# Sliding-window attention beside a gated linear unit: row maxima sent two units later, a second scratch buffer, and another order inside the PV burst

## The chip, the core and the metric

The kernel runs on one core of one Trainium2 chip. What is measured is the device time of one execution in microseconds (us). A core has a matrix engine (TensorE, PE in the profile; PEld is its weight load), a vector engine (VectorE, DVE), a scalar engine (ScalarE, ACT), a general engine (GpSimd, POOL), and a queue that issues nearly all DMAs here (SyncE, SP). Each engine executes its own list of instructions in order and waits on semaphores for the others.

## The reference

Two branches share the input x (2048 rows of 512) and are mixed row by row by a gate.

```python
def _A_ref(x, wqkv, wo):
    H = 32; Dh = 16; W = 256
    q, k, v = ...                                   # x @ wqkv, 32 heads of 16
    scores = jnp.einsum("bhqd,bhkd->bhqk", q, k) * (Dh ** -0.5)
    mask = (idx[:, None] - idx[None, :] >= 0) & (idx[:, None] - idx[None, :] < W)
    p = _softmax(jnp.where(mask, scores, -1e9))
    return einsum("bhqk,bhkd->bhqd", p, v) ... @ wo

def _B_ref(x, w_gate, w_up, w_down):                # F = 1376
    return (_sigmoid(x @ w_gate) * (x @ w_up)) @ w_down

g = _sigmoid((x * gate_w).sum(-1, keepdims=True))
return g * a + (1 - g) * b
```

Everything is float32. A query sees itself and the 255 keys before it, so a block of 128 queries needs three blocks of 128 keys.

## The kernel before, in words

The 32 heads are taken in 8 groups of 4, the 2048 rows in 16 blocks of 128. One pair (head group, block) is a *unit*; units are numbered `u` from 0 to 127, and the main loop runs over them and a few more. Four consecutive units are a *group of maxima* with index `s`, 32 in all. The engines' order is the order in which this Python loop emits instructions: TensorE, VectorE, ScalarE and SyncE are not reordered.

In the loop, unit `u` does the following:

- `s_part(u, hh)`, for each of the four heads `hh`: the scores of query block `u` with its three key blocks, queries on partitions (tile `s`, two PSUM buffers). VectorE adds the mask and takes the row maximum (L314); the elementwise result goes into a scratch tile `junk` that nobody reads, the maximum into `mx`.
- `st_part(u - 9, hh)`: the transposed scores of key block `u - 9` with query blocks `u - 9` to `u - 7` (tile `st`, three PSUM buffers). Here the contraction has extra rows, in which the query side carries minus the row maximum, so that the exponential on ScalarE (L360) comes out shifted. Block `u - 7` is thus the newest whose maximum is read. A key block at the end of a head group reads only up to that group's end.
- For this the maxima of four units are turned into ring rows. `max_split(s)` makes a high and a low part and transposes them on VectorE (L324, L325, L329, tiles `nm` and `nt`); `max_store(s)` writes them to DRAM with four DMAs (L335); `max_load(s)` reads them back into row 0 of the `ring`'s 32-row strips with one DMA (L340).
- `pv_burst(w, n)`: probabilities times values for `n` query blocks at once (four, near the end two), at the head of unit `w + n + 10`: that is every unit with `u % 4 == 2` in the steady part. Each matmul uses a tile of 64 rows by 32 columns of the array: two halves of the key rows (`half`) times four heads. `acc[0]`, tag `s`, collects the first half, `acc[1]`, tag `st`, the second. Key halves `k` have different widths, from 64 to 320 query columns. `o_take` then copies one half out on ScalarE (L422), adds the other on VectorE (L425), and appends four `oT` stores and one of the sums to the list `later`.
- Fill work: `run_slots` emits matmuls of the gate and up projections (`gu`) and of later q/k projections (`pj`) between the attention matmuls, the two row halves offset against each other. Their results are copied out and appended to `later` as `gu_scratch` stores.
- SyncE's list in a unit: `max_store` if due, then all that `later` holds from the unit before, then up to three DMAs that build the next `ring` stack (`sdma`: copies from `sh` and `sl`), then `max_load` if due. `sdma` is filled with thirteen DMAs in units with `u % 8 == 1`.

After the attention part the down projection and the output projection follow; the change does not touch them.

Of the kernel before, what the change touches and what calls it, by code (L numbers as in the profile page):

```python
# [7 lines left out]
F32 = mybir.dt.float32  # L8
# [6 lines left out]
P = 128  # L15
# [9 lines left out]
NB = T // P  # L25
# [3 lines left out]
VW = DH + 1  # L29
VROW = H * VW  # L30
GW = HG * VW
# [25 lines left out]
def gated_mix_kernel(  # L57
# [14 lines left out]
    mm = nc.tensor.matmul  # L72
# [34 lines left out]
    NU = NG * NB  # L107
# [20 lines left out]
    with ExitStack() as actx:  # L128
# [169 lines left out]
        def s_part(u, hh):  # L298
            g, i = divmod(u, NB)
            s = g * NC + i // 4  # L300
            if i % 4 == 0 and hh == 0:
                mxs[s] = spool.tile([P, HG, 4], F32, tag="mx", name=f"mx{s}")
            k0 = max(0, i - 2)
            tag = "st" if u < LAG and hh >= 2 else "s"
            pt = ps.tile([P, 3 * P], F32, tag=tag, name=f"s{u}_{hh}", bufs=2 if tag == "s" else 3)
            lhsT = blk(g, i, hh, 0)
            for k, e in pieces(g, k0, i + 1):
                mm(  # L308
                    pt[:, (k - k0) * P:(e - k0) * P], lhsT, blk(g, k, hh, 1, e - k),
                    start=k == k0, stop=e == i + 1, skip_group_check=True,  # L310
                )
            n = (i + 1 - k0) * P
            junk = spool.tile([P, 3 * P], F32, tag="junk", name=f"junk{u}_{hh}", bufs=1)
            nc.vector.tensor_tensor_reduce(  # L314
                junk[:, 0:n], pt[:, 0:n], mask[:, 3 * P - n:], scale=1.0, scalar=NEG,
                op0=ALU.add, op1=ALU.max, accum_out=mxs[s][:, hh, i % 4:i % 4 + 1],
            )
# [3 lines left out]
        def max_split(s):  # L321
            mx = mxs.pop(s)
            nm = spool.tile([P, HG, 2, 4], F32R, tag="nm", name=f"nm{s}")
            nc.vector.tensor_scalar(nm[:, :, 0], mx, -1.0, None, op0=ALU.mult)  # L324
            nc.vector.scalar_tensor_tensor(  # L325
                nm[:, :, 1], mx, -1.0, nm[:, :, 0].bitcast(F32), op0=ALU.mult, op1=ALU.subtract,
            )
            nms[s] = spool.tile([P, QB], F32, tag="nt", name=f"nt{s}")
            nc.vector.transpose(nms[s], nm.bitcast(F32).rearrange("p h l b -> p (h l b)"))  # L329
# [14 lines left out]
        pts = {}  # L344
# [40 lines left out]
        def pv_burst(u, n):  # L385
            g, i = divmod(u, NB)
            acc = [
                ps.tile([P, CH], F32, tag=tag, name=f"pv{tag}{u}", bufs=bufs)
                for tag, bufs in (("s", 2), ("st", 3))
            ]  # L390
            span = {
                k: (max(0, 64 * k), min(n * P, 64 * k + 5 * 64))
                for k in range(-4, 2 * n) if i + k // 2 >= 0
            }
            order = [
                sorted((k for k in span if k % 2 == half), key=lambda k: (span[k][0] - span[k][1], k))
                for half in range(2)
            ]
            for m in range(len(order[0])):
                for hh in range(HG):  # L400
                    for half in range(2):
                        k = order[half][m]
                        j = i + k // 2
                        q0, q1 = span[k]
                        o = -(k // 2) * P
                        r = slice(64 * half, 64 * half + 64)
                        c = j * GW + hh * VW
                        mm(  # L408
                            acc[half][32 * hh:32 * hh + 32, q0:q1],
                            vg[g % 2][r, c:c + 32], pts[g * NB + j][r, hh, q0 + o:q1 + o],  # L410
                            start=m == 0, stop=m == len(order[0]) - 1, skip_group_check=True,
                            tile_position=(64 * half, 32 * hh),
                        )
            o_take(g, i, n, acc)

        def o_take(g, i, n, acc):
# [212 lines left out]
        for u in range(N):  # L629
            if u == LAG:  # L630
                vctx.close()
                ppool = actx.enter_context(tc.tile_pool(name="ppool", bufs=1))
                for k in range(2):
                    vg.append(ppool.tile([P, NB * GW + 16], F32, name=f"vg{k}"))
                    nc.gpsimd.memset(vg[k][:, NB * GW:], 0.0)
                hvs += [
                    v.rearrange("p (w t) -> p w t", t=CH)
                    for v in [vg[0][:, 0:2 * CH]] + [region[:, o:o + 2 * CH] for o in HVO]
                ]
            if u == LAG + 1 or u % NB == 0 and 0 < u < NU:  # L640
                v_load(u // NB)
            if u == 4:
                load_gu(0, 0)
                load_gu(0, 1)
            if u % 8 == 1 and u > 8 and u // 8 + 1 < NP:
                sdma = stack_build(u // 8 + 1)
            if u % 16 == 8 and u // 16 + 2 < NG:
                raw_q = load_wqk(u // 16 + 2)
            if u % 4 == 0 and 0 < u <= NU:
                max_store(u // 4 - 1)  # L650
            run_dmas(later)
            later.clear()
            run_dmas(sdma[:SD])
            del sdma[:SD]
            if u % 4 == 1 and 1 < u <= NU + 1:
                max_load(u // 4 - 1)
            if WD <= u < WD + 16 and (u - WD) % 2 == 0:
                load_d((u - WD) // 2)
            s4 = {1: 4, 5: 5, 9: 6, U_LAST: NSTEP - 2, U_LAST + 1: NSTEP - 1}.get(u)
            if u % 4 == 3 and u > LAG and (u + 2) // 4 + 4 < NSTEP - 2:  # L660
                s4 = (u + 2) // 4 + 4
            if s4 is not None:
                if u < LAG:
                    (work if u == 1 else first).append((3 * ND, lambda k, s4=s4: proj_mm(s4, k), lambda s4=s4: proj_post(s4)))
                else:
                    work.append(proj_group(s4))
            if u == NU + PVLAG - 1:
                hold_group(*rest.pop(0))
            for hh in range(HG):
                if hh == 0 and u % 2 == 0:  # L670
                    if u in bursts:
                        pv_burst(*bursts[u])
                if hh == 0:
                    head = min(2, bursts.get(u, (0, 0))[1] // 2)
                    run_slots(head)
                if u < NU:
                    s_part(u, hh)
                if 0 <= u - LAG < NU:
                    st_part(u - LAG, hh ^ 1 if u < NU else hh)
                if u < LAG:  # L680
                    flush(behind)
                else:
                    if behind:
                        behind.pop(0)()
                    if acts:
                        acts.pop(0)()
                if u >= LAG and (hh < HG - 1 or u % 2 == 0 if u < NU else hh % 2 == 1):
                    run_slots((GAP if u < NU else 2 * GAP) - (hh < head if u < NU else head * (hh == 1)))
            if u < LAG - 1:
                done += run_first(n_first * (u + 1) // LAG - done)  # L690
            elif u < LAG:
                run_first(n_first - done - 3 * ND)
                split_gu(0, 0)
                split_gu(0, 1)
                flush(acts)
                flush(behind)
                run_first(3 * ND)
                done = 0
            if u % 4 == 3 and u < NU:
                max_split(u // 4)  # L700
            if u // 16 + 2 < NG:
                if u % 16 == 13:
                    acts.append(lambda g=u // 16 + 2, r=raw_q: (
                        split_wqk(g, r, 0), behind.append(lambda: split_wqk(g, r, 1))))
            if 0 <= u - LAG < NU:
                mask_p(u - LAG)
            if WD + 2 <= u < WD + 10 and (u - WD) % 2 == 0:
                acts.append(lambda f=(u - WD) // 2 - 1: split_d(f, True))
            if SUMS <= u and (u - SUMS) % 4 == 0:
                sums_load((u - SUMS) // 4)  # L710
            if SUMS + 2 <= u and (u - SUMS) % 4 == 2:
                behind.append(lambda c=(u - SUMS) // 4: later.append(sums_invert(c)))
            if u >= HLOAD and (u - HLOAD) % 2 == 0:
                h_load((u - HLOAD) // 2)
            if u >= N - 2:
                flush(acts)
                flush(behind)
                h_skew(u - N - 1)
# [162 lines left out]
```

## Time and profile before

| | |
|---|---|
| median of 3 runs | 766.97 us (766.41 to 768.11) |
| profiled execution | 765.99 us, span 764.3 us |
| busy: TensorE, VectorE, ScalarE, GpSimd | 745.9, 483.6, 434.9, 163.7 us |
| share of the last chain: TensorE, VectorE | 81%, 9% |
| `junk` reductions (L314) | 512, 270.8 us busy |
| `pv` matmuls (L408) | 2880, each in two float32 passes counted apart: 1440 on `pvs`, 1440 on `pvst` |

The span runs from the first to the last instruction. "Busy" is time in which at least one instruction of the engine runs; a busy TensorE can still have one half of its rows empty. The attention part, where all of the change lies, goes from about 40 to 590 us.

### The profile page before, as it was taken

Reading aid. Unit: us, or ns where it says so; the run is one execution under the profiler, and the core shown is the slowest. Engines: PE = TensorE matmul, PEld = TensorE weight load, DVE = VectorE, ACT = ScalarE, POOL = GpSimd, SP = SyncE. Lnnn points to the kernel's source line nnn. Section 1 sums busy time; section 2 is a strip of 40 time slices with the busy share of each in tenths; the row PEclk is TensorE's granted clock in tenths of the full one; section 3 lists DMA queues with packets and bytes.
Section 4 is the critical chain, followed back from the end, with each engine's and each line's share of the span. In section 5 each row is a group of like instructions: output and inputs, shape, how many; then the busy total and the mean of one; then the engine's idle time right before and its main releaser. Section 6 shows DMA issues by size and latency. Waiting matters only on the chain.

```text
span 764.3 us, 20558 instructions
## 1 busy us (share of the span) xinstructions
PE 745.9 (98%) x7652; PEld 592.4 (78%) x7652; DVE 483.6 (63%) x1429; ACT 434.9 (57%) x900; POOL 163.7 (21%) x256
## 2 busy tenths in 40 slices
PE   8999999999999999999999999999999999999997
PEld 6877777877877777878787777878877778888886
DVE  5356767766676766777667677577612794739371
ACT  5412666666576666666656666666665673625341
POOL 7000322233133232323223322332331000000000
PEclk9999999999999999999999999999999999999999
DMA  8373544445344455344543525643366776648351
GB/s 301 93 240 123 143 123 116 124 114 158 118 117 128 122 138 140 101 135 113 148 140 99 149 66 144 165 123 107 101 196 186 234 245 224 185 142 269 110 163 55
DMA packets 88787, 112.69 MB, mean 147 GB/s; under 512 B 36082, under 2 KB 45810, under 8 KB 88688
## 3 DMA queue, kind: packets, MB, share of 16 engines
q1 hardware_dynamic: 88688, 111.39, 49.7%
q8 instruction: 60, 0.98, 0.6%
q14 instruction: 39, 0.32, 0.1%
HBM read 49.72 MB, written 36.45 MB: 113 GB/s over the span
## 4 chain that ended last, share of the span: by engine, by line
PE 81%; DVE 9%; DMA 4%; SPq 3%; issue 2%; ACT 1%; DVEq 0%; ACTq 0%
PE gu L240 29%; PE pvs L408 8%; PE pj L240 7%; PE s L308 7%; PE st L355 4%; PE pd L81 4%; PE pd L79 4%; PE pd L80 4%; DVE junk L314 4%; PE vps L79 2%; SPq L282 2%; PE vps L80 2%; PE vps L81 2%; PE pa L79 2%; PE pa L81 2%
## 5 line engine op out<-in xcount | busy, mean ns | idle before, releaser
L314 DVE CUSTOM_DVE_ANT_0 junk<-s,mask 128x384 f32<-128x384 f32 (+2 forms) x512 | 270.8, 529 | 157.5 <-PE st L355 74.8
L240 PE MATMUL gu<-xh,w 64*128 64x512 f32 (+3 forms) x1384 | 353.7, 394 | 0.4 <-ACT sp L501 0.3
L360 ACT ACTIVATE region<-st 128x384 f32<-128x384 f32 (+2 forms) x512 | 237.9, 475 | 126.2 <-PE st L355 71.9
L240 PE MATMUL gu<-xl,w 64*128 64x512 f32 (+3 forms) x692 | 243.8, 394 | 0.0
L240 PEld LDWEIGHTS gu<-xh,w 64*128 64x128 f32 (+3 forms) x1384 | 203.6, 183 | 16.6 <-ACT sp L501 1.4
L308 PE MATMUL s<-ring 64*128 64x384 f32 (+2 forms) x536 | 168.0, 338 | 10.7 <-DVE mx L314 9.3
L355 PE MATMUL st<-ring 64*128 64x384 f32 (+2 forms) x536 | 169.1, 334 | 0.0
L365 POOL TENSOR_SCALAR_AFFINE_SELECT region<-region 128x512 f32<-128x512 f32 x128 | 82.9, 648 | 362.0 <-ACT region L360 305.6
L308 PEld LDWEIGHTS s<-ring 64*128 64x128 f32 x536 | 94.0, 184 | 56.3 <-DVE mx L314 45.1
L240 PEld LDWEIGHTS gu<-xl,w 64*128 64x128 f32 (+3 forms) x692 | 124.5, 183 | 9.7 <-issue 1.6
L355 PEld LDWEIGHTS st<-ring 64*128 64x128 f32 x536 | 94.7, 184 | 6.1
L240 PE MATMUL pj<-xh,wqh 64*128 64x512 f32 (+1 forms) x232 | 93.4, 405 | 1.0 <-ACT xh L75 1.0
L240 PE MATMUL pj<-xl,wqh 64*128 64x512 f32 (+1 forms) x232 | 91.8, 399 | 0.0
L408 PE MATMUL pvs<-region,vg 64*32 64x320 f32 (+4 forms) x1440 | 74.5, 346 | 0.0
L408 PE MATMUL pvst<-region,vg 64*32 64x320 f32 (+4 forms) x1440 | 73.1, 341 | 0.0
L240 PE MATMUL pj<-xh,wql 64*128 64x512 f32 (+1 forms) x232 | 72.5, 398 | 0.0
L370 POOL TENSOR_SCALAR_AFFINE_SELECT region<-region 128x512 f32<-128x512 f32 x112 | 71.5, 638 | 0.0
L81 PE MATMUL pd<-ring,hb 128*128 128x512 f32 (+1 forms) x176 | 69.4, 394 | 0.7 <-DVE hb L76 0.7
L408 PEld LDWEIGHTS pvs<-region,vg 64*32 64x32 f32 x1440 | 49.7, 106 | 26.0 <-issue 9.6
L79 PE MATMUL pd<-ring,hb 128*128 128x512 f32 (+1 forms) x176 | 69.4, 394 | 0.0
L80 PE MATMUL pd<-ring,hb 128*128 128x512 f32 (+1 forms) x176 | 68.8, 391 | 0.4 <-DVE ring L121 0.4
L501 ACT COPY sp<-gu 128x512 f32<-128x512 f32 (+2 forms) x88 | 51.3, 584 | 2.4 <-PE gu L240 2.4
(76 smaller groups left out, 979.8 us busy)
## 6 DMA issues: line engine op xcount, KB each, us to landing
gu_scratch<-sp SPq DMA_DIRECT2D x80, 256.0 KB
region<-gu_scratch SPq DMA_DIRECT2D x68, 256.0 KB
ring<-sh SPq DMA_DIRECT2D x128, 128.0 KB
ring<-sl SPq DMA_DIRECT2D x64, 128.0 KB
guraw<-in_wgu_dram SPq DMA_DIRECT2D x20, 256.0 KB
v_scratch<-region SPq DMA_DIRECT2D x16, 272.0 KB
vg<-v_scratch SPq DMA_DIRECT2D x8, 544.0 KB
region<-in_xT_dram SPq DMA_DIRECT2D x16, 256.0 KB
```

The costliest lines, as they stand in the source:

```text
L79: mm(ps, lh, rh, start=first, stop=False)
L80: mm(ps, lh, rl, start=False, stop=False)
L81: mm(ps, ll, rh, start=False, stop=last)
L240: mm(pt[0:fw], (wl if w == 2 else wh)[r, d], (xl if w == 1 else xh)[r, d, c * CH:(c + 1) * CH], start=k == 0 and half != 1, stop=k == 3 * ...
L308: mm(pt[:, (k - k0) * P:(e - k0) * P], lhsT, blk(g, k, hh, 1, e - k), start=k == k0, stop=e == i + 1, skip_group_check=True,)
L314: nc.vector.tensor_tensor_reduce(junk[:, 0:n], pt[:, 0:n], mask[:, 3 * P - n:], scale=1.0, scalar=NEG, op0=ALU.add, op1=ALU.max, accum_out ...
L355: mm(pt[:, (q - j) * P:(e - j) * P], lhsT, blk(g, q, hh, 0, e - q), start=q == j, stop=e == last, skip_group_check=True,)
L360: nc.scalar.activation(pts[u][:, hh, 0:n], pt[:, 0:n], AF.Exp, scale=SCALE)
L365: nc.gpsimd.affine_select(p[:, :, 0:P], p[:, :, 0:P], pattern=[[0, HG], [1, P]], compare_op=ALU.is_ge, fill=0.0, base=0, channel_multiplie ...
L370: nc.gpsimd.affine_select(p[:, :, 2 * P:], p[:, :, 2 * P:], pattern=[[0, HG], [-1, P]], compare_op=ALU.is_gt, fill=0.0, base=0, channel_mu ...
L408: mm(acc[half][32 * hh:32 * hh + 32, q0:q1], vg[g % 2][r, c:c + 32], pts[g * NB + j][r, hh, q0 + o:q1 + o], start=m == 0, stop=m == len(or ...
L501: nc.scalar.copy(t[0:width(f, w)], gp.pop((f, c, w))[0:width(f, w)])
```

## The change

Three edits.

1. `junk` has two buffers. In the order of instructions VectorE no longer waits for its own preceding result ahead of a reduction.
2. `max_split(s)` is emitted at the end of unit 4s+5 in place of unit 4s+3, directly ahead of the burst that opens unit 4s+6. `max_store(s)` goes from unit 4s+4 to 4s+6 and `max_load(s)` from 4s+5 to 4s+7.
3. In the burst, the two row halves no longer take key halves of the same width at the same time. Each half alternates between its widest and its narrowest remaining key half, one starting wide, the other narrow; all twelve are then emitted in the order of the columns that their half has done before, four heads at a time.

```diff
-            junk = spool.tile([P, 3 * P], F32, tag="junk", name=f"junk{u}_{hh}", bufs=1)
+            junk = spool.tile([P, 3 * P], F32, tag="junk", name=f"junk{u}_{hh}", bufs=2)
...
-            order = [
-                sorted((k for k in span if k % 2 == half), key=lambda k: (span[k][0] - span[k][1], k))
-                for half in range(2)
-            ]
-            for m in range(len(order[0])):
+            order = []
+            for half in range(2):
+                ks = sorted((k for k in span if k % 2 == half), key=lambda k: (span[k][0] - span[k][1], k))
+                at = 0
+                for m in range(len(ks)):
+                    k = ks.pop(-1 if m % 2 != half else 0)
+                    order.append((at, half, m, len(ks) == 0, k))
+                    at += span[k][1] - span[k][0]
+            for _, half, m, last, k in sorted(order):
+                j = i + k // 2
+                q0, q1 = span[k]
+                o = -(k // 2) * P
+                r = slice(64 * half, 64 * half + 64)
                 for hh in range(HG):
-                    for half in range(2):
-                        k = order[half][m]
...
-                            start=m == 0, stop=m == len(order[0]) - 1, skip_group_check=True,
+                        start=m == 0, stop=last, skip_group_check=True,
...
-            if u % 4 == 0 and 0 < u <= NU:
+            if u % 4 == 2 and 2 < u <= NU + 2:
                 max_store(u // 4 - 1)
...
-            if u % 4 == 1 and 1 < u <= NU + 1:
+            if u % 4 == 3 and 3 < u <= NU + 3:
                 max_load(u // 4 - 1)
...
-            if u % 4 == 3 and u < NU:
-                max_split(u // 4)
+            if u % 4 == 1 and 1 < u <= NU + 1:
+                max_split(u // 4 - 1)
```

What this does to the order is shown for group 13 (units 52 to 55). SyncE before, from the store of its maxima (`nt13`) to the stack copies of unit 59; `ob11` is the result of the burst at the head of unit 58:

```order
L335 DMA max_scratch<-nt13_4146 32x32 x4
L282 DMA gu_scratch<-sp3_2_0_4117 128x512
L282 DMA gu_scratch<-sp3_3_0_4193 128x512
L282 DMA ring_63<-fill_scratch 4x2x1024
L282 DMA ring_63<-sh16_3805 32x1024 x2
L340 DMA ring_63<-max_scratch 4x2x512
L476 DMA guraw4_1_4258<-in_wgu_dram 128x512
L282 DMA gu_scratch<-sp3_0_1_4256 128x512
L282 DMA ring_63<-sh16_3805 32x1024 x3
L282 DMA oT_scratch<-ob11_4327 16x512 x4
L282 DMA sum_scratch<-ob11_4327 4x512
```

And SyncE after, the same stretch:

```order
L282 DMA gu_scratch<-sp3_2_0_4117 128x512
L282 DMA gu_scratch<-sp3_3_0_4184 128x512
L282 DMA ring_63<-fill_scratch 4x2x1024
L282 DMA ring_63<-sh16_3805 32x1024 x2
L478 DMA guraw4_1_4248<-in_wgu_dram 128x512
L335 DMA max_scratch<-nt13_4264 32x32 x4
L282 DMA gu_scratch<-sp3_0_1_4246 128x512
L282 DMA ring_63<-sh16_3805 32x1024 x3
L282 DMA oT_scratch<-ob11_4326 16x512 x4
L282 DMA sum_scratch<-ob11_4326 4x512
L282 DMA ring_63<-sh16_3805 32x1024 x3
L340 DMA ring_63<-max_scratch 4x2x512
```

The store now stands ahead of the burst's `oT` stores, and the load behind them and behind three more stack copies. In both versions the first `st` that reads group 13 is that of key block 50, head 1, in unit 59.

VectorE before, around the split of group 13 (`junk55_3` is the last reduction of unit 55):

```order
L314 ISA junk55_3_4138,mx13_3863<-s55_3_4136,mask_155 128x384
L314 ISA mx13_3863 128x1
L324 TENSOR_SCALAR nm13_4143<-mx13_3863 128x4x4
L325 SCALAR_TENSOR_TENSOR nm13_4143<-mx13_3863,nm13_4143 128x4x4
L329 STREAM_TRANSPOSE nt13_4146<-nm13_4143 128x32
L314 ISA junk56_0_4159,mx14_4156<-s56_0_4157,mask_155 128x384
```

VectorE after, the same three operations:

```order
L314 ISA junk57_3_4256,mx14_4147<-s57_3_4254,mask_155 128x384
L314 ISA mx14_4147 128x1
L324 TENSOR_SCALAR nm13_4261<-mx13_3854 128x4x4
L325 SCALAR_TENSOR_TENSOR nm13_4261<-mx13_3854,nm13_4261 128x4x4
L329 STREAM_TRANSPOSE nt13_4264<-nm13_4261 128x32
L314 ISA junk58_0_4334,mx14_4147<-s58_0_4332,mask_155 128x384
```

They went from between units 55 and 56 to between units 57 and 58, where TensorE's burst stands between the reductions' matmuls.

More of the change, by code (lines that the diff above doesn't have):

```diff
@@ L394, in pv_burst @@
             }
-            order = [
-                sorted((k for k in span if k % 2 == half), key=lambda k: (span[k][0] - span[k][1], k))
-                for half in range(2)
-            ]
-            for m in range(len(order[0])):
-                for hh in range(HG):
-                    for half in range(2):
-                        k = order[half][m]
[L403 to L410, printed above, removed]
-                            start=m == 0, stop=m == len(order[0]) - 1, skip_group_check=True,
-                            tile_position=(64 * half, 32 * hh),
-                        )
+            order = []
[11 more added lines that the diff above has]
+                r = slice(64 * half, 64 * half + 64)
+                for hh in range(HG):
+                    c = j * GW + hh * VW
+                    mm(
+                        acc[half][32 * hh:32 * hh + 32, q0:q1],
+                        vg[g % 2][r, c:c + 32], pts[g * NB + j][r, hh, q0 + o:q1 + o],
+                        start=m == 0, stop=last, skip_group_check=True,
+                        tile_position=(64 * half, 32 * hh),
+                    )
             o_take(g, i, n, acc)
```

## The prediction

> **What bounds the kernel now.** I read the page first, then the waits, then one stretch of four units on three engines.
>
> ```profile
> span 764.3 us, 20558 instructions
> PE 745.9 (98%) x7652; PEld 592.4 (78%) x7652; DVE 483.6 (63%) x1429; ACT 434.9 (57%) x900; POOL 163.7 (21%) x256
> PE 81%; DVE 9%; DMA 4%; SPq 3%; issue 2%; ACT 1%; DVEq 0%; ACTq 0%
> ```
>
> TensorE is busy for 98% of the span and carries 81% of the chain that ended last; VectorE carries 9%. So whatever makes TensorE wait is paid in full, and what only frees VectorE pays at most where TensorE waits for it. These are the rows of that wait, from the groups by line between 90 and 560 us (the second number after the bar is idle time just before the group):
>
> ```profile
> L308 PEld LDWEIGHTS s<-ring 64*128 64x128 f32 x483 | 88.3, 184 | 51.5 <-DVE mx L314 43.7
> L308 PE MATMUL s<-ring 64*128 64x384 f32 (+2 forms) x483 | 156.6, 334 | 10.5 <-DVE mx L314 9.1
> ```
>
> The `s` matmul waits for one of its two PSUM buffers, which the maximum at L314 gives back. The array is wholly idle for 10.5 us, the weight loads for 51.5; in between, one row half runs alone.
>
> Now the stretch that the change touches: unit 57's last reduction, the burst at the head of unit 58 (it starts at 268.51, called T below), and the first `st` of unit 59. The rows are TensorE's and VectorE's timeline, then SyncE's queue.
>
> ```profile
> 268.51 0.43 PE L408 MATMUL pvs<-region,vg 64*32 64x320 f32 x1
> ...
> 274.50 0.33 PE L355 MATMUL st<-ring 64*128 64x384 f32 x1
> ...
> 269.04 0.08 DVE L314 DVE_READ_ACCUMULATOR2_ANT mx<- 128x1 f32 x1
> 263.32 1.69 SPq L335 DMA_DIRECT2D max_scratch<-nt  x4
> ...
> 267.91 0.58 SPq L340 DMA_DIRECT2D ring<-max_scratch  x1
> ...
> 269.01 0.44 SPq L282 DMA_DIRECT2D gu_scratch<-sp  x1
> 269.49 2.19 SPq L282 DMA_DIRECT2D ring<-sh  x3
> 273.02 1.71 SPq L282 DMA_DIRECT2D oT_scratch<-ob  x4
> 274.78 0.55 SPq L282 DMA_DIRECT2D sum_scratch<-ob  x1
> 275.37 1.75 SPq L282 DMA_DIRECT2D ring<-sh  x3
> ```
>
> Each row has its start, its length, the engine, the line and, last, how many instructions it merges. What to see: the maxima of group 13 (units 52 to 55) are stored at 263.32 and loaded into the ring at 267.91. The first matmul that reads them is `st` of key block 50 in unit 59, at 274.50: its queries are units 50 to 52. So today there are 6.6 us between the load's issue and its reader.
>
> **The moved split (with its DMAs).** The split, four stores and one load go two units later, but the reader stays in unit 59. The load is now issued at the head of unit 59, behind everything that SyncE is given in unit 58. I add that queue up from T.
>
> VectorE is done with unit 57 at 269.12, T+0.6. The three split operations follow:
>
> ```profile
> L325 DVE SCALAR_TENSOR_TENSOR nm<-mx,nm 128x16 fp32r<-128x16 f32 x32 | 13.2, 413 | 1.1
> L324 DVE TENSOR_SCALAR nm<-mx 128x16 fp32r<-128x16 f32 x32 | 12.6, 395 | 0.9
> L329 DVE STREAM_TRANSPOSE nt<-nm 128x32 f32<-128x32 f32 x32 | 6.8, 211 | 1.1
> ```
>
> They take 0.41+0.40+0.21 = 1.0 us, in VectorE's pause under the burst: T+1.7. Four stores, 1.7: T+3.4. One `gu_scratch` store, 0.45: T+3.9. Three `sh`, 1.75 to 2.2: T+5.8. The `oT` stores came at 273.02, T+4.5, since they wait for the burst's result; now they stand behind the stores and start at T+5.8: 1.75, T+7.5. The sums, 0.6: T+8.1. Three more `sh`, 1.75: T+9.9. The load's issue, 0.6: T+10.5. Its landing has no row. The nearest is a small DMA that the queue itself waited for, in a stretch where the DMA engines were full; here they are under half busy (a wait of SyncE's queue in total, times, longest; then two rows of the table by windows, whose last three numbers are the granted clock, the DMA engines' share and GB/s):
>
> ```profile
> SPq L214 <- DMA fill_scratch<-fr: 2.5, 1, 2.5
> 16.50:19.00 2.50, 2.50 (x13) 2.04 (x12) 0.00 (x0) 0.59 (x1) 0.00 (x0) 1.00 0.93 347
> 246.00:262.00 16.00, 15.41 (x214) 12.01 (x212) 11.06 (x38) 9.82 (x22) 4.86 (x8) 1.00 0.41 115
> ```
>
> I take 2.0 us (bounds 1.0 and 2.5): T+12.5. TensorE wants the rows at 274.50, T+6.0. It stands for 6.5 us, and behind it in its order everything else: `s`, the gate and up matmuls, later bursts. Nothing covers it, because all engines are fed by TensorE. With the queue's place left as it was the answer would hardly change: the last `sh` before the load ends at 277.12 even today, 2.6 us after the reader.
>
> This holds for groups 3, 5, ..., 27, whose unit also carries `sh` copies (the next stack is built in units 8k+1 to 8k+5). Group 1 has no burst and no `oT`, but six `sh`; I count it the same. That is 14 × 6.5 = 91 us.
>
> Groups 2, 6, ..., 30, and 29 and 31, have no `sh` there. The case of group 14, burst at 284.32:
>
> ```profile
> 284.32 0.45 PE L408 MATMUL pvs<-region,vg 64*32 64x320 f32 x1
> 289.95 0.41 PE L355 MATMUL st<-ring 64*128 64x384 f32 x1
> 288.27 1.71 SPq L282 DMA_DIRECT2D oT_scratch<-ob  x4
> 290.03 0.57 SPq L282 DMA_DIRECT2D sum_scratch<-ob  x1
> ```
>
> Split, stores and one `gu` store reach T+3.9 as before; `oT` was ready at T+3.95 and stays; the sums end at 290.60, T+6.3; the load's issue T+6.9, landed T+8.9; the reader is at T+5.6. Stall 3.3 us, ten times: 33 us. Groups 4, 8, ..., 28 begin a head group; their first reader comes two units later (key block 16k reads only from its own group on), and since four units take 15.8 us, from 268.51 to 284.32, that is well behind T+8.9: nothing. Stalls together: 124 us.
>
> **What the split and the second buffer give back.** Without the own-result wait, reductions may follow each other closely:
>
> ```profile
> 244.18 0.08 DVE L314 DVE_READ_ACCUMULATOR2_ANT mx<- 128x1 f32 x1
> 244.18 0.69 DVE L266 TENSOR_TENSOR sl<-pr,sh 128x512 fp32r<-128x512 f32 x1
> ...
> 248.06 0.56 DVE L314 CUSTOM_DVE_ANT_0 junk<-s,mask 128x384 f32<-128x384 f32 x1
> 248.54 0.08 DVE L314 DVE_READ_ACCUMULATOR2_ANT mx<- 128x1 f32 x1
> 248.77 0.56 DVE L314 CUSTOM_DVE_ANT_0 junk<-s,mask 128x384 f32<-128x384 f32 x1
> ```
>
> From 248.06 to 248.77 is 0.71 a reduction, 0.15 of it after the accumulator is read; an instruction with no such wait started at 244.18 together with the read. Some 0.2 us less for each, and the split's 1.0 us out of the unit where VectorE is late. It pays only where TensorE waits for `mx`: between 9.1 (array idle) and 43.7 us (loads idle). I take the middle, 27, and keep both ends.
>
> **The mixed burst.** Same 48 matmuls and same columns, 1280 for each row half; ordered so that the two halves stay level. If each half runs its own list, this costs and gives nothing: 0.
>
> **The clock.** After a stop TensorE may come back slower. The start and the end of this trace show it:
>
> ```profile
> 9.71 0.63 PE L240 MATMUL pj<-xh,wqh 128*128 128x512 f32 x1
> 10.14 0.69 PE L240 MATMUL pj<-xl,wqh 128*128 128x512 f32 x1
> ...
> 11.65 0.39 PE L79 MATMUL vps<-w,xh 128*128 128x512 f32 x1
> 11.87 0.40 PE L80 MATMUL vps<-wvl,xh 128*128 128x512 f32 x1
> 760.06 0.39 PE L81 MATMUL pa<-xh,xl 128*128 128x512 f32 x1
> 764.00:766.00 2.00, 0.00 (x0) 0.00 (x0) 0.00 (x0) 0.00 (x0) 0.00 (x0) 0.79 0.00 0
> ```
>
> Equal matmuls start 0.43 us apart at 10 us and 0.22 apart from 11.65 on. The last one ends at 760.45, and the granted clock, 0.79 on average from 764 to 766, is one half for 0.84 us of these two: it fell at about 765.2, 4.7 us after the last matmul. A stop of 6.5 us is longer than that, one of 3.3 is not. How long the half clock then lasts no row shows; work that goes on for 4 us at half speed costs 2 us. 14 × 2 = 28 us, with bounds 0 and 14 × 3.4 = 48.
>
> [...]
>
> **The sum.** The profiled execution took 765.99 us (span 764.3 and 1.7 around it), 1 us under the median of 766.97. 766 + 91 + 33 - 27 + 28 = 891 us.
>
> **Rivals.**
>
> *The stalls without the clock.* If the clock is kept, 891 - 28 = 863 us. For it: no stop within the work of this trace is long enough to tell.
>
> *The maxima arrive in time.* Then nothing is late, VectorE's relief is all that is left, and the time is 766 - 27 = 739 us. It needs the load landed by T+6.0, 6.5 us earlier than I add up; it would decide from the point where the load is issued by T+3.4, which is where the four stores end. Against it: `oT` stands ahead of the load in the same queue and cannot start before T+4.5.
>
> *The row halves are not free of each other.* Then a narrow matmul beside a wide one wastes its half's time: the six pairs would take 4 × 320 + 2 × 256 = 1792 columns in place of 1280. What a column costs is read from one burst in which the halves are unequal (burst at a head group's first unit):
>
> ```profile
> 157.04 0.43 PE L408 MATMUL pvs<-region,vg 64*32 64x320 f32 x1
> 157.31 0.43 PE L408 MATMUL pvs<-region,vg 64*32 64x320 f32 x1
> ...
> 157.91 0.31 PE L408 MATMUL pvst<-region,vg 64*32 64x64 f32 x8
> 158.01 0.42 PE L408 MATMUL pvs<-region,vg 64*32 64x128 f32 x8
> ```
>
> A pass of 320 columns takes 0.27 us, two passes 0.54, so 512 more columns take 0.86 us; 30 bursts, 26 us on top: 917. Against it: the 64-wide matmuls of the second half start at 157.91, before the 128-wide ones of the first half that stand ahead of them in the program; the halves do run apart.
>
> [...]
>
> *The change does little.* If the reader did not need these rows (or the load overtook the queue) and VectorE's relief were hidden as well: 766.
>
> **How the numbers follow.** Stalls with the clock: 0.64. Stalls with the clock kept: 0.23. Halves in lockstep on top: 0.05. Stalls half as long as I say, about 810: 0.03. In time, faster: 0.04. No change: 0.01. Forecast 890. Low end: 14 × 5.5 + 10 × 2.3 = 100 of stalls, less 36, no clock: 830. High end: landing 2.5 makes 14 × 7.0 + 10 × 3.8 = 136; less 20, plus 38 it is 920, and 930 takes in most of the lockstep case. A measurement of this kernel can tell 0.2% from no change. Slower 0.95, same 0.01, faster 0.04.
>
> **What would show it.** The groups and waits of the changed kernel should have `st` at L355 idle for a DMA of `ring<-max_scratch`, about 24 times, up to 6 or 7 us, 100 us or more together, and none in units that begin a head group; PE's busy share should fall to 85 to 90%, and the granted clock under 1 right after the long stops. L314 should repeat every 0.5 to 0.6 us where it is fed, and the wait of `s` for `mx` nearly vanish. Bursts should still take 2.2 us from first to last start. I am wrong if the load's issue in SyncE's queue comes ahead of the `oT` stores, if `st` does not wait for it, or if the bursts grow.

## The result, and the profile after

The changed kernel takes 928.17 us in the median of four runs (926.85 to 933.63), the kernel before 767.34 us beside it on the same chip: a ratio of 1.211, 95% interval 1.206 to 1.216. Forecast were 890 us and a range of 830 to 930: the direction and the cause hold, the size is 38 us short and lies just under the top of the range. The profiled execution has a span of 926.2 us, against 764.3 before: 161.9 us more.

These lines of the page answer to those of before; the last but one is the granted TensorE clock in tenths, in 40 slices.

```profile
span 926.2 us, 20215 instructions
PE 788.9 (85%) x7652; PEld 659.1 (71%) x7652; DVE 473.9 (51%) x1429; ACT 435.9 (47%) x900; POOL 163.9 (18%) x256
PEclk9999889798989979897988889798998999999999
PE 74%; SPq 10%; DMA 9%; DVE 4%; issue 2%; ACT 1%; DVEq 0%; ACTq 0%
```

TensorE fell from 98% to 85% busy; SyncE's queue and the DMAs, 7% of the last chain before, have 19% of it. But TensorE is also busy for longer, 788.9 against 745.9 us, with the same 7652 instructions: so part of its own work became slower. The next row is from the table of waits (us in total, times, longest).

```profile
PE st L355 <- DMA ring<-max_scratch: 128.8, 24, 7.4
```

And from the groups by line between 90 and 730 us, which here hold about as many `s` matmuls as 90 to 560 us did before:

```profile
L355 PE MATMUL st<-ring 64*128 64x384 f32 (+2 forms) x514 | 175.1, 357 | 128.8 <-DMA ring<-max_scratch 128.8
L308 PE MATMUL s<-ring 64*128 64x384 f32 (+2 forms) x491 | 156.1, 344 | 0.0
L308 PEld LDWEIGHTS s<-ring 64*128 64x128 f32 x491 | 96.5, 202 | 19.9 <-DVE mx L314 12.9
```

`st` stands 24 times, 128.8 us in all, for the load of the maxima. In return the wait of `s` for `mx` is mostly gone: the array is never wholly idle for it (10.5 us before), the weight loads wait 12.9 us for `mx` where they waited 43.7. And a mean matmul at L308 takes 344 ns where it took 334; the granted clock, under 1 in many slices, is the likely reason, which e6 puts to the test: one of 384 columns takes 0.52 us at 113.59, where the granted clock is 0.50, and 0.33 us at 107.31, where it is 1.00.

One cycle shows the stop, group 13 again. Its burst starts at 326.37 (T). TensorE's timeline:

```profile
326.37 0.47 PE L410 MATMUL pvs<-region,vg 64*32 64x320 f32 x4
...
328.86 0.50 PE L240 MATMUL gu<-xh,w 64*128 64x512 f32 x1
...
332.47 0.33 PE L308 MATMUL s<-ring 64*128 64x384 f32 x1
339.61 0.65 PE L355 MATMUL st<-ring 64*128 64x384 f32 x1 [6.81 <-DMA ring<-max_scratch]
```

SyncE's queue in the same stretch:

```profile
328.07 2.57 SPq L335 DMA_DIRECT2D max_scratch<-nt  x4
330.74 0.37 SPq L282 DMA_DIRECT2D gu_scratch<-sp  x1
331.15 1.76 SPq L282 DMA_DIRECT2D ring<-sh  x3
333.01 1.91 SPq L282 DMA_DIRECT2D oT_scratch<-ob  x4
334.97 0.55 SPq L282 DMA_DIRECT2D sum_scratch<-ob  x1
335.56 1.76 SPq L282 DMA_DIRECT2D ring<-sh  x3
337.37 0.58 SPq L340 DMA_DIRECT2D ring<-max_scratch  x1
```

Nothing is between 332.80 and 339.61 on TensorE. The queue runs without a gap of more than 0.1 us from the first store, at T+1.7, to the load, whose issue ends at T+11.6, and the reader starts 1.7 us after that.

### The profile page after: what moved, and what is told of

It reads as the page before. It is cut to its first block, busy times and chain, and to the rows that moved or that the text cites. A ratio compares the mean times of both kernels' runs of the same rounds, so it can differ in the third digit from the quotient of the medians.

```text
span 926.2 us, 20215 instructions
## 1 busy us (share of the span) xinstructions
PE 788.9 (85%) x7652; PEld 659.1 (71%) x7652; DVE 473.9 (51%) x1429; ACT 435.9 (47%) x900; POOL 163.9 (18%) x256
## 4 chain that ended last, share of the span: by engine, by line
PE 74%; SPq 10%; DMA 9%; DVE 4%; issue 2%; ACT 1%; DVEq 0%; ACTq 0%
PE gu L240 28%; PE pj L240 9%; SPq L282 9%; DMA ring<-max_scratch 6%; PE st L355 5%; PE s L308 5%; PE pvst L410 4%; PE pd L81 3%; PE pd L79 3%; PE pd L80 3%; PE pvs L410 3%; DMA region<-gu_scratch 2%; PE vps L79 2%; DVE junk L314 2%; PE vps L80 2%
## 5 line engine op out<-in xcount | busy, mean ns | idle before, releaser
L240 PE MATMUL gu<-xh,w 64*128 64x512 f32 (+3 forms) x1384 | 386.8, 427 | 0.3 <-ACT sp L503 0.3
L355 PE MATMUL st<-ring 64*128 64x384 f32 (+2 forms) x536 | 180.8, 356 | 128.8 <-DMA ring<-max_scratch 128.8
L240 PE MATMUL gu<-xl,w 64*128 64x512 f32 (+3 forms) x692 | 260.8, 420 | 0.0
L240 PEld LDWEIGHTS gu<-xh,w 64*128 64x128 f32 (+3 forms) x1384 | 228.7, 202 | 17.4 <-issue 6.6
L355 PEld LDWEIGHTS st<-ring 64*128 64x128 f32 x536 | 107.0, 207 | 140.2 <-issue 124.1
L308 PE MATMUL s<-ring 64*128 64x384 f32 (+2 forms) x536 | 164.7, 347 | 0.0
L240 PEld LDWEIGHTS gu<-xl,w 64*128 64x128 f32 (+3 forms) x692 | 133.2, 197 | 12.3 <-issue 5.8
L308 PEld LDWEIGHTS s<-ring 64*128 64x128 f32 x536 | 100.8, 201 | 24.0 <-DVE mx L314 13.2
L240 PE MATMUL pj<-xh,wqh 64*128 64x512 f32 (+1 forms) x232 | 103.7, 452 | 1.5 <-ACT xh L75 1.5
L240 PE MATMUL pj<-xl,wqh 64*128 64x512 f32 (+1 forms) x232 | 100.5, 439 | 0.0
L240 PEld LDWEIGHTS pj<-xh,wqh 64*128 64x128 f32 (+1 forms) x232 | 50.3, 218 | 4.0 <-ACT xh L75 2.3
```

The costliest lines, as they stand in the source:

```text
L240: mm(pt[0:fw], (wl if w == 2 else wh)[r, d], (xl if w == 1 else xh)[r, d, c * CH:(c + 1) * CH], start=k == 0 and half != 1, stop=k == 3 * ...
L308: mm(pt[:, (k - k0) * P:(e - k0) * P], lhsT, blk(g, k, hh, 1, e - k), start=k == k0, stop=e == i + 1, skip_group_check=True,)
L355: mm(pt[:, (q - j) * P:(e - j) * P], lhsT, blk(g, q, hh, 0, e - q), start=q == j, stop=e == last, skip_group_check=True,)
```

## The experiments

Eleven kernels ran. Each ratio is to the kernel before on the same chip. The theory was the recorded sum: stops by the order of SyncE's queue, plus a half clock after them, less VectorE's relief. Its rivals were that the burst's new order makes part of the loss, that the second buffer makes most of the gain or none, and that the clock follows from the stops but costs little.

### Each edit alone

*e1: the second buffer.*

```diff
-  junk = spool.tile([P, 3 * P], F32, tag="junk", ..., bufs=1)
+  junk = spool.tile([P, 3 * P], F32, tag="junk", ..., bufs=2)
```

> The kernel before with only the second buffer for junk. Theory: VectorE's reductions follow each other in about 0.5 us in place of 0.71 where they are fed, and TensorE's waits for mx shrink, also in the unit behind the split; the time falls by some 20 us, to 740 to 757. Rival: the relief is hidden behind TensorE, or the wait comes from the split alone; then 765 to 768.

762.38 us, ratio 0.9931 (0.9917 to 0.9945): about 5 us faster. That was less than expected. VectorE's timeline says why:

```profile
241.28 0.55 DVE L314 CUSTOM_DVE_ANT_0 junk<-s,mask 128x384 f32<-128x384 f32 x1
241.75 0.08 DVE L314 DVE_READ_ACCUMULATOR2_ANT mx<- 128x1 f32 x1
241.75 0.55 DVE L314 CUSTOM_DVE_ANT_0 junk<-s,mask 128x384 f32<-128x384 f32 x1
...
245.66 0.17 DVE L324 TENSOR_SCALAR nm<-mx 128x16 fp32r<-128x16 f32 x1
245.87 0.51 DVE L325 SCALAR_TENSOR_TENSOR nm<-mx,nm 128x16 fp32r<-128x16 f32 x1
246.41 0.21 DVE L329 STREAM_TRANSPOSE nt<-nm 128x32 f32<-128x32 f32 x1
246.55 0.52 DVE L314 CUSTOM_DVE_ANT_0 junk<-s,mask 128x384 f32<-128x384 f32 x1
```

So do the groups by line between 90 and 560 us:

```profile
L308 PE MATMUL s<-ring 64*128 64x384 f32 (+2 forms) x485 | 154.3, 331 | 8.2 <-DVE mx L314 7.0
L308 PEld LDWEIGHTS s<-ring 64*128 64x128 f32 x484 | 88.5, 184 | 45.6 <-DVE mx L314 37.3
```

The mechanism works: a reduction starts 0.47 us after the one before it, together with the read of the other's accumulator (0.71 before). But the wait of TensorE hardly shrinks: 37.3 of 43.7 us are left. The split still sits between two reductions, here from 245.66 to 246.55; how much of the wait is its doing, e9 shows below.

*e3: the order inside the burst.* The burst's part of the change, nothing else.

```diff
+                    k = ks.pop(-1 if m % 2 != half else 0)
+                    order.append((at, half, m, len(ks) == 0, k))
...
+            for _, half, m, last, k in sorted(order):
...
                 for hh in range(HG):
-                    for half in range(2):
```

> The kernel before with only the new order in the burst. Theory: the two halves run apart, so the columns cost the same; but the burst now ends with wide matmuls in place of narrow ones, and the trace of the changed kernel has the next matmul 2.48 us after the burst's start in place of 2.38; 34 bursts, 3 us more: 769 to 772. Rival one: no difference, 767. Rival two, lockstep halves: 793.

770.55 us, ratio 1.0034 (1.0021 to 1.0047): slower by 2.6 us. A burst and the fill work behind it, here and in the kernel before, each from TensorE's timeline:

```profile
254.57 0.47 PE L410 MATMUL pvs<-region,vg 64*32 64x320 f32 x4
...
257.06 0.50 PE L240 MATMUL gu<-xl,w 64*128 64x512 f32 x1
```

```profile
252.68 0.45 PE L408 MATMUL pvs<-region,vg 64*32 64x320 f32 x1
...
255.06 0.50 PE L240 MATMUL gu<-xl,w 64*128 64x512 f32 x1
```

2.49 against 2.38 us. Over the whole trace, the time from a burst's first start to the next other matmul is 2.48 against 2.38 us in 22 long bursts, 1.94 against 1.88 in the eight that open a head group, and 1.41 against 1.30 in four short ones: 3.1 us in all.

*e4: both without the move.* The diffs of e1 and e3 together.

> The changed kernel without the moved split: second junk buffer and new burst order. Theory: the two add up, about 20 us less and 3 us more: 745 to 758. Rival: the loss does not sit in the move, and this one stays above 800.

765.35 us, ratio 0.9964 (0.9951 to 0.9977). The sum of the two holds (0.9931 × 1.0034 = 0.9965); the expectation was too fast only because it still priced the second buffer too high.

*e2: the move alone.* One buffer and the old burst.

```diff
-            if u % 4 == 0 and 0 < u <= NU:
+            if u % 4 == 2 and 2 < u <= NU + 2:
                 max_store(u // 4 - 1)
...
-            if u % 4 == 1 and 1 < u <= NU + 1:
+            if u % 4 == 3 and 3 < u <= NU + 3:
                 max_load(u // 4 - 1)
...
-            if u % 4 == 3 and u < NU:
-                max_split(u // 4)
+            if u % 4 == 1 and 1 < u <= NU + 1:
+                max_split(u // 4 - 1)
```

> The kernel before with only the split, the store and the load of the maxima moved. Theory: it holds the whole loss: 24 stops of st, about 129 us together as in the changed kernel, some 45 us of halved clock behind them, and 5 to 15 us back because the split leaves the unit where VectorE is late: 920 to 945. Rival: what the changed kernel lost beyond its 129 us of stops comes from the new order of the burst or from junk, not from the clock: then about 885.

917.72 us, ratio 1.1936 (1.1910 to 1.1961), with the stops of the changed kernel:

```profile
PE st L355 <- DMA ring<-max_scratch: 128.2, 24, 7.7
```

So the move alone makes nearly the whole slowdown. What the other two edits add to it is not sharp: 13 us by the two ratios, 7.4 us by the spans of the two profiled executions (918.8 and 926.2), while executions of one of these kernels lie 6 to 7 us apart. In the two traces the burst accounts for 3.1 us and the clock for about 6.8: in the attention part TensorE is busy at half clock for 83.2 us here and for 96.8 in the change, by the clock's records. About half of that is lost: in the change, `gu` matmuls of 512 columns in one row half start 0.43 us apart at half clock (677.67, 678.09, 678.52) and 0.23 us apart at the full one (107.48, 107.71, 107.94). The second buffer's 5 us cannot be read from so small a difference.

### The stop: what in the queue makes it

*e5: load right behind the store, everything else as in the change.*

```diff
             if u % 4 == 2 and 2 < u <= NU + 2:
                 max_store(u // 4 - 1)
+                max_load(u // 4 - 1)
...
-            if u % 4 == 3 and 3 < u <= NU + 3:
-                max_load(u // 4 - 1)
```

> The changed kernel with the load of the maxima issued directly behind their store, ahead of the oT stores and the sh copies. Theory (the queue's order sets the stops): the load waits only for the store's landing, is issued about 5 us after the burst's start and landed at 7 to 7.5, against a reader at 6.0: 24 stops of 1 to 1.5 us, 30 us together, none long enough for the clock; 767 + 30 - 18 + 3 = 782. Rival: the way through DRAM itself takes that long; then the stops stay at 3 us and more and the time above 840.

784.03 us, ratio 1.0208 (1.0192 to 1.0223), near the 782 of the theory.

```profile
PE st L355 <- DMA ring<-max_scratch: 23.3, 20, 4.4
```

Of 128.8 us of stops 23.3 are left, and the span is 144.4 us shorter (781.8 against 926.2). The store, the split and the burst stand where the change put them; only one DMA of 0.58 us issue time went past the others in the queue. The stops that are left have another source. In group 13, whose burst starts here at 280.01, the queue stands between store and load, and over all loads together it waits for the stores to land:

```profile
281.71 2.70 SPq L335 DMA_DIRECT2D max_scratch<-nt  x4
285.55 0.57 SPq L340 DMA_DIRECT2D ring<-max_scratch  x1
SPq L340 <- DMA max_scratch<-nt: 38.9, 52, 3.0
```

The load starts 5.5 us after the burst, 1.1 us after the last store's issue. In the change this wait is hidden behind the twelve DMAs between the two.

*e7: only the six `sh` copies out from between store and load.*

```diff
-            run_dmas(sdma[:SD])
-            del sdma[:SD]
...
                 max_load(u // 4 - 1)
+            if u % 8 != 2:
+                run_dmas(sdma[:SD])
+                del sdma[:SD]
```

> The changed kernel with the six sh copies taken out from between the store and the load (none in units 8k+2, and those of 8k+3 behind the load). Theory: the groups with sh copies then stop as long as the others, 3 us in place of 6 to 7, 75 us together; such stops seldom halve the clock, 10 us; 767 + 75 + 10 - 18 + 3 = 837. Rival: the odd groups stop long for another reason, and the time stays above 900.

877.12 us, ratio 1.1434 (1.1395 to 1.1473): 40 us more than was expected.

```profile
PE st L355 <- DMA ring<-max_scratch: 83.8, 24, 5.4
```

The stops did shrink, by 45 us. In the 14 groups whose stop was 5.7 to 7.4 us it became 2.5 to 4.1; all 24 together are 9 us over the 75 expected. What did not shrink as expected is the half clock: TensorE was still busy at half clock for 75.4 us in the main loop, so about 38 us were lost to it, not 10. A stop of 2.96 us (the one that ends at 163.09) was followed by half the clock too, from 164.55 on; the last section shows when.

### The clock

*e6: work for TensorE during the stop.* Directly ahead of each late `st` but one, 28 or 14 dummy matmuls of 384 columns write into the PSUM buffer that this `st` then overwrites; the order of all DMAs stays.

```diff
+            if hh == 1 and u % 4 == 2 and u % 16 != 14 and u + LAG < NU:
+                for _ in range(28 if u % 8 == 2 else 14):
+                    mm(pt, xh[:, 0, 0:P], xh[:, 0, 0:3 * P], start=True, stop=True)
```

> The changed kernel with idle work for TensorE: ahead of each st that has to wait it runs 28 (groups with sh copies) or 14 matmuls of 384 columns into the PSUM buffer that this st then overwrites, about 4.5 and 2.3 us; outputs are unchanged. Theory: the load lands when it did, so the stops last as long with the matmuls counted in, but the clock stays at one, and the 97 us that TensorE worked at half clock (48 us of loss) go: about 880. Rival: the loss beyond the stops does not come from the clock; 928 or, with work added, more.

893.15 us, ratio 1.1625 (1.1599 to 1.1651). The extra work makes the kernel faster than the change by 37 us (1.211 - 1.1625, of 767). In 17 of the 24 places `st` still waits for the DMA behind the dummy work, so the stop ends no earlier there; what changes is what follows it. TensorE's time at half clock falls from 96.8 to 18.7 us, by the clock's records and the matmuls in them: half of each, 48.4 and 9.4 us, is put down as lost, a difference of 39. So the cost of the half clock is not just read from records: taking most of it away gives back about that time, 37 us.

### The gain, with the stops out of the way

*e8: split under the burst and the maxima still in time.* In the kernel before, the lag between `s` and `st` goes from 9 to 11 units. The burst, which goes with the lag, then opens unit 4s+4, right behind the split at the end of unit 4s+3; the first reader moves to unit 4s+9, while store and load stay in units 4s+4 and 4s+5. The stack copies begin two units later, four in a unit; `FIRST` takes the place of `LAG` in the start-up code, which so stays as it was. The second buffer is in.

```diff
-LAG = 9
+FIRST = 9
+LAG = 11
...
-SD = 3
+SD = 4
...
-            junk = spool.tile(..., bufs=1)
+            junk = spool.tile(..., bufs=2)
...
-            if u % 8 == 1 and u > 8 and u // 8 + 1 < NP:      # next ring stack
+            if u % 8 == 3 and u > 8 and u // 8 + 1 < NP:
```

> The kernel before with the second junk buffer and the transposed scores 11 units behind in place of 9 (the stack copies start two units later, four a unit). The split stays at the end of unit 4s+3, but the burst now opens unit 4s+4, so the split lies under a burst, and the first reader of its maxima is in unit 4s+9, five units on. Theory: the split's relief without a stop: TensorE's 37 us of weight loads waiting for mx nearly vanish, and of the 762 of the second buffer alone some 10 to 17 go: 745 to 752. Rival: TensorE's own work already bounds those units, 760 or more; the copies being later could also stop s.

745.36 us, ratio 0.9709 (0.9692 to 0.9726): the fastest kernel of this study, 22 us under the one before. And with one buffer only (e9):

```diff
-            junk = spool.tile(..., bufs=2)
+            junk = spool.tile(..., bufs=1)
```

> The version with the transposed scores 11 units behind, with one junk buffer as before. It tells the two parts of its gain of 22 us apart. Theory: the split under a burst is the larger part, the second junk buffer is worth about 5 us as it was alone: 749 to 753. Rival: the gain needs both, and with one buffer it stays near 762.

750.07 us, ratio 0.9774 (0.9752 to 0.9795). The waits in the groups by line between 90 and 560 us, with two buffers and with one:

```profile
L309 PE MATMUL s<-ring 64*128 64x384 f32 (+2 forms) x484 | 147.5, 322 | 0.1
L309 PEld LDWEIGHTS s<-ring 64*128 64x128 f32 x484 | 88.8, 184 | 20.9 <-DVE mx L315 11.3
```

```profile
L309 PEld LDWEIGHTS s<-ring 64*128 64x128 f32 x484 | 88.8, 184 | 24.2 <-DVE mx L315 14.1
```

The split's place under the burst takes the wait for `mx` from 43.7 to 14.1 us and is worth about 17 us (2.26% of 767); the second buffer takes another 2.8 us of that wait and is worth 5. The longer lag and the later stack copies were not run without the split under the burst, so the 17 us hold for all three together.

### The burst: which part of its order costs

Two kernels with one run each, with the old placement and one buffer. The first (e10) keeps equal widths side by side but gives each row half its four heads in a row; the second (e11) keeps the heads' old alternation and puts narrow beside wide.

```diff
-                for hh in range(HG):
-                    for half in range(2):
+                for half in range(2):
+                    for hh in range(HG):
```

> The kernel before with the burst's key halves paired by equal width as before, but emitted four heads of one row half at a time, as the changed kernel does. Theory one (the runs of four cost the 0.1 us a burst): next matmul 2.48 us after a burst's start, time about 770. Theory two (narrow beside wide costs it): 2.38 us and 767.

```diff
+            for half in range(2):
+                ks = order[half]
+                order[half] = [ks.pop(-1 if m % 2 != half else 0) for m in range(len(ks))]
```

> The kernel before with the burst's key halves paired narrow beside wide as in the changed kernel, but emitted with the two row halves alternating head by head, as before. Theory one (the runs of four cost it): 2.38 us from a burst's start to the next matmul. Theory two (narrow beside wide, with wide matmuls at the end): 2.48 us and about 770.

765.75 and 772.35 us, beside 767.11 for the kernel before. A burst and the next fill work in each, fours first:

```profile
252.50 0.47 PE L408 MATMUL pvs<-region,vg 64*32 64x320 f32 x4
...
254.87 0.49 PE L240 MATMUL gu<-xl,w 64*128 64x512 f32 x1
```

```profile
254.17 0.45 PE L411 MATMUL pvs<-region,vg 64*32 64x320 f32 x1
...
256.70 0.49 PE L240 MATMUL gu<-xl,w 64*128 64x512 f32 x1
```

2.37 us and 2.53, where 2.38 was before. So the runs of four cost nothing, and the new pairing does. But the pairing also changes the end of a burst: it closes with matmuls of 192 and 256 columns, where the old order closes with 64. The traces point there. In the long bursts the last start comes 2.18 us after the first in e3, 2.24 in e11 and 2.23 before, while from the last start to the next other matmul it takes 0.30, 0.27 and 0.15 us. A mixed order that ends narrow was not run, so this stays an argument.

## Why the prediction was right, and where it was off

**What bounds the kernel.** Right. TensorE's stops were paid in full: e5 takes 105.5 us of stops away and the span falls by 144.4; the rest, 38.9, is most of what the half clock no longer costs: TensorE works 6.0 us of the attention part at half clock in place of 96.8, and half of the difference is 45. The mean clock goes from 0.922 to 0.993 over the span.

**The queue behind the move.** Right, place and order. In group 13 the first store was forecast for T+1.7 and came at T+1.7. The end of the load's issue was forecast for T+10.5 and came at T+11.6: the four stores took 2.57 us in place of 1.7, and the `oT` stores 0.2 more. The landing was taken as 2.0 and was 1.7 at most (337.95 to 339.61); and TensorE came to the reader at T+6.4, not T+6.0. The 14 stops in units with `sh` copies add up to 92.0 us where 91 was forecast, the ten without to 36.8 where 33 was. None stands in a group that begins a head group. Together 128.8 against 124.

**The clock.** This step was mis-sized, 28 us in the sum where about 48.4 were lost (half of the 96.8 us at half clock), and one sentence in it was wrong: "A stop of 6.5 us is longer than that, one of 3.3 is not." The long stops all halved the clock and lost 35 us, 2.5 each where 2 was taken; seven of the ten short ones did it too and lost the other 13. The 4.7 us between the last matmul and the clock's fall at the end of the trace before was read as a stop's least length. It was one sample of a grid's phase, a bound from above only: that fall came 754.35 us after the start of the trace's first clock record, 221 times 3.413 us, on a grid of the kind that the last section shows. No run shows the 3.4 us a stop of the step's upper bound, nor the 38 us in the range's top; in the runs a long stop cost those 2.5. And where 4 us of work at half speed were taken, the changed kernel has 2.9 to 5.9 us behind a long stop, 5.0 in the mean.

**What the split and the second buffer give back.** 27 was taken, the middle of 9.1 to 43.7. Where it can be measured without the stops it is about 22 us, 17 with the split under the burst and 5 for the buffer (e8, e9, e1). In the change itself only the remainder tells: 161.9 - 128.8 - 48.4 - 3.1 leaves -18.4. That the reductions would repeat every 0.5 to 0.6 us was right (0.47); that this is where TensorE waits was mostly not, since e1 left 37.3 of 43.7 us standing; with the split moved as well, 14.1 us are left with one buffer and 11.3 with two (e9, e8).

**The mixed burst.** 0 was taken. "Bursts should still take 2.2 us from first to last start" holds, with 2.18; what the forecast left out is that the next matmul then starts later, 0.10 us for a long burst and 3.1 us in all. The lockstep rival gave 0.86 us for a burst and is out.

So of the 38 us that are missing, the clock makes 20, the relief 9, the stops 5, the burst 3; the last one is that the sum came to 891 and was written as 890. All four missed in the same direction. That 928 still lies inside the range is in part luck: its top was raised from 920 to 930 for the lockstep of the row halves, which did not happen. TensorE's busy share, forecast at 85 to 90%, is 85%.

**The rivals.** The one without the clock, 863 us, is out by e6: with most of the half clock gone it is 893, since the stops were a little longer and the relief smaller. For maxima in time, 739 us were named, and a load issued by T+3.4, where the four stores were thought to end. Behind these stores that point is out of reach: in e5, with the load next to them, those of group 13 end at T+4.4 and the load starts at T+5.5, when they have landed, a wait for which the prediction has no term. So e5 still stops 20 times, up to 4.4 us. e8 has the maxima in time, by another way, and comes to 745.

## What to carry to other kernels

Ahead of moving a producer, add up the queue that its DMAs stand in, from the point where its data is ready to the first reader: here a load of 0.58 us behind up to sixteen other issues cost 128.8 us of stops, and moving that one instruction back past up to twelve of them returned 144. Add the wait for a store to land where a load reads it back: 1.1 us stood there in e5. To hide small work under a burst, move the reader with it (here by a longer lag), and the same idea that lost 161 us gains 22. Price each stop of TensorE above its own length: 48 us came on top of 129 here.

## What the hardware showed that was not expected

The records of the granted clock follow fixed stretches. Apart from the last of each trace, the half-clock records are 3.41, 6.83 or 10.24 us long, one, two or three times 3.413, at places on one grid in a trace; the full-clock records between them are 17.07, 30.72 or 34.13 us in the changed kernel, five, nine or ten times that. The clock also fell after stretches that were not wholly idle, one of them with 1.45 us of work. Two pairs of neighbouring stretches, of the changed kernel and of e7, from the table by windows (length, busy time of TensorE, its weight loads, VectorE, ScalarE, GpSimd, then the granted clock, DMA share and GB/s):

```profile
109.80:113.21 3.41, 1.45 (x14) 1.48 (x16) 0.13 (x1) 0.59 (x2) 0.20 (x1) 1.00 0.64 142
113.22:116.63 3.41, 3.41 (x22) 3.38 (x20) 1.61 (x7) 1.94 (x5) 0.04 (x1) 0.50 0.35 104
```

```profile
430.80:434.21 3.41, 1.62 (x15) 1.66 (x17) 0.31 (x1) 1.12 (x3) 0.11 (x1) 1.00 0.48 111
434.22:437.62 3.40, 3.39 (x33) 2.76 (x31) 2.93 (x11) 2.61 (x6) 1.22 (x2) 1.00 0.73 205
```

In the first pair TensorE is busy 1.45 us, idle 1.96, and the next stretch has half the clock though it is full of work. In the second it is busy 1.62, idle 1.79, and the next stretch keeps the clock. In the changed kernel, from 80 us on, the 21 full-clock stretches that a half one followed were idle for 1.83 us or more, the 183 that a full one followed for 1.68 or less. Over it, e2, e5, e6 and e7 together, every full-clock stretch with at least 1.86 us idle was followed by a half one and every one with at most 1.80 by a full one; between, both occur. A half-clock stretch was followed by a full one when 0.56 us of it or less were idle, and by another half one from 0.67 on. In the first 15 us two stretches do not fit (a full one of e5 with 1.62 us idle was followed by a half one, a half one of e7 with 0.42 by another); why stays open. So length alone does not tell whether a stop of 2 to 4 us costs clock; its place in the grid does here: the first pair's stop was 3.09 us long, and a stop of 3.14 us (ending at 196.74) cost none.
